# The tail of a pooled-attention and adapter kernel: where the last gates and one output addition are computed

## The chip, the cores and the metric

The kernel runs on one core of a Trainium2 chip. The metric is the device time of one execution in microseconds (us), lower is better. A core has five engines that work side by side and meet at semaphores: TensorE (PE, with its weight loads as PEld), VectorE (DVE), ScalarE (ACT), GpSimd (POOL) and SyncE (SP), which here issues the DMA transfers.

## What is computed

Two steps follow one another. The first is attention against pooled keys, where keys and values are the same matrix; the second is a mixture of eight small adapters, of which each token uses its two best. Cut to what matters:

```python
kv_pool = kv.reshape(B, H//4, 4, W//4, 4, C).mean(axis=(2, 4))     # 768 rows of 128 per batch
k = v = kv_pool.reshape(B, -1, C) @ w_sr
a = softmax(q @ k.T / sqrt(C));  x = a @ v                          # B*N = 4*12288 tokens, C = 128
logits = x @ w_gate                                                 # E = 8 adapters
w = softmax(the 2 largest logits)
out = x + sum over those 2 of  w_e * ((x @ A[e]) @ B[e])            # rank 16
```

## The kernel before

The 49152 tokens are worked in 96 chunks of 512 tokens; a chunk is four slices of 128 tokens (NS = 4). The code calls the last chunk `n` (95). Each chunk goes through these stages, and several chunks are in flight at once:

- `scores`: TensorE multiplies keys and queries, ScalarE takes the exponential (L303, L304).
- `weigh`: TensorE multiplies the exponentials with the values, extended by the gate's eight columns and a column of ones (L315). Attention output, logits and the softmax denominator come out of one product.
- `normalise` (L322, L326, L333), called `tops4` in the tail (L793, L794, L799): VectorE divides by the denominator and takes the sorted logits of each token with MAX8.
- gates: the weight of the better of two adapters is a sigmoid of the difference of logits, done as a tanh. `gate` (L342 to L346) works on GpSimd for a pair of chunks; ScalarE takes the tanh; a 1 is added; adapters that were not chosen get zero.
- `gated_hidden` (L416, L419) or, for the last six chunks, `down`/`hidden` (L430, L778) and the multiplication with the gates, `apply_gate` (L442) or `gated` (L753) on VectorE: the adapters' inner products times the gates.
- `turn` or `turned`: TensorE transposes (L762, L381), and ScalarE or VectorE copies the result out of PSUM (L768, L770, L390).
- `up` (L462): TensorE multiplies with B. Then the output is x plus this: either VectorE adds in one step from PSUM (`add_rows`, L476), or ScalarE copies PSUM to SBUF (`take`, L467) and GpSimd adds x in SBUF (`add`, L471), or TensorE puts x into the PSUM bank first (`x_first`, L454) and a `take` finishes it.
- `put` (L481) sends 256 KB of output from SyncE's queue.

The schedule is written out by hand: the order of the calls in the source is the order of the instructions in each engine's own queue, and nothing is moved by a planner. Inside the main loop chunks up to 89 take their gates through a 16-bit buffer `gw_all` which is sent to DRAM and read back in another layout. The last six chunks (90 to 95) use them straight from SBUF: `gate_tanhs(p)` for pairs 45 and 46 (chunks 90 to 93) writes the tanh to a 32-bit tile `th`, and GpSimd adds 1 and writes it into `gw_all`, whose layout has the adapters outside and the slices inside, so that the eight gates of a token lie 16 bytes apart. Chunks 94 and 95 use 32-bit tiles `arg4` and `arg5` (named `r` in the trace) in which a token's eight gates lie side by side.

After the loop stands the tail, in which the last chunks are finished in an order of its own. For the last chunk, `gate_args` (L734 to L737) forms the tanh's argument and the mask, `gate_tanh` (L740) the tanh and `gate_w` the weight: on VectorE one instruction (L745), on GpSimd two (L747, L748). `gate_args` and `gate_w` take the engine as an argument. At the end `tail_ok` (L547 to L549, GpSimd) and `all_ok` (L553 on TensorE, L554 and L556 on VectorE) write the flag `bad`, which every engine loads (L881) to decide on a branch that is not taken here; then the program ends.

```python
    gate_args(n, 0, NS, nc.vector, top5, arg5, msk5)
    gate_tanh(0, NS, arg5)
    up(n - 3, mtile([P, NTOK], name="d2"))
    gated(n - 1, 0, NS, arg4, h4)
    o2 = take(n - 3)
    ...
    gate_w(0, NS, nc.vector, arg5, msk5)
    ...
    gated(n, 0, NS, arg5, h5)
    for c, o in ((n - 6, o6), (n - 5, o0), (n - 4, o1), (n - 3, o2)):
        add(c, o, nc.gpsimd)
        put(c, o)
        if c == n - 4:
            put(n - 2, o3)
    tail_ok()
```

Of the kernel before, what the change touches and what calls it, by code (L numbers as in the profile page):

```python
# [16 lines left out]
ALU = mybir.AluOpType  # L17
# [4 lines left out]
def kernel(  # L22
# [10 lines left out]
    nc = tc.nc  # L33
# [8 lines left out]
    NS = NTOK // P  # L42
# [248 lines left out]
    tt, xps, xpair, xn, gw, gin, xT, hg, hgT, hps = {}, {}, {}, {}, {}, {}, {}, {}, {}, {}  # L291
# [63 lines left out]
    def gate_tanhs(p):  # L355
        gw[p] = gw_all[:, p % 4].rearrange("p e s -> p s e")
        if p < OWN // 2:
            nc.scalar.activation(gw_all[:, p % 4], garg[p].rearrange("p s e -> p e s"), AF.Tanh,
                                 bias=0.0, scale=0.5)
        else:  # L360
            th = small.tile([P, 2 * NS, E], FP32, tag="th", name="th")
            nc.scalar.activation(th, garg[p], AF.Tanh, bias=0.0, scale=0.5)
            nc.gpsimd.tensor_scalar(gw[p], th, 1.0, None, op0=ALU.add)

# [90 lines left out]
    def up(c, bank=None):  # L457
        fresh = c not in dps
        if fresh:
            dps[c] = mtile([P, NS, P], name="d_ps") if bank is None else as_tokens(bank)  # L460
        for s in range(NS):
            mm(dps[c][:, s], columns(hgT[c], c, s), b_bf, start=(s == 0 and fresh),  # L462
               stop=(s == NS - 1), skip_group_check=True)

    def take(c, lo=0, hi=NS):
        osb = half_out()
        nc.scalar.activation(osb[:, lo:hi], dps[c][:, lo:hi], AF.Copy)  # L467
        return osb

    def add(c, osb, eng):  # L470
        eng.tensor_tensor(osb, osb, xn[c][:, :, 0:C], op=ALU.add)  # L471

    def add_rows(c, lo=0, hi=NS, osb=None, bank_=None):
        osb = half_out() if osb is None else osb
        d = dps[c][:, lo:hi] if bank_ is None else bank_
        nc.vector.tensor_tensor(osb[:, lo:hi], d, xn[c][:, lo:hi, 0:C], op=ALU.add)  # L476
        return osb

    def put(c, osb, lo=0, hi=NS, queue=None):
        t0 = c * NTOK  # L480
        (queue or nc.sync).dma_start(  # L481
            out[t0:t0 + NTOK, :].rearrange("(p s) c -> p s c", p=P)[:, lo:hi], osb[:, lo:hi])
# [17 lines left out]
    def half_out():  # L500
        if not spare:
            o = run.tile([P, 2, NS, P], FP32, tag="osb", name="osb", bufs=3)
            spare.extend([o[:, 0], o[:, 1]])
        return spare.pop(0)
# [41 lines left out]
    def tail_ok():  # L546
        nc.gpsimd.tensor_scalar(ok[:, tail], rv[:, tail], 1.0 / L_HI, None, op0=ALU.is_ge)  # L547
        nc.gpsimd.tensor_scalar(low, rv[:, tail], 1.0 / L_LO, None, op0=ALU.is_le)
        nc.gpsimd.tensor_tensor(low, low, ok[:, tail], op=ALU.mult)  # L549
# [102 lines left out]
    for c in range(2, NCH - 1):  # L652
# [17 lines left out]
        if c >= 3 and c % 2 == 1:  # L670
            gate_tanhs((c - 3) // 2)
# [54 lines left out]
    def bank(i):  # L726
        return ps_e.tile([P, NTOK], FP32, tag=f"e{i}", name=f"e{i}")

    def gate_args(c, lo, hi, eng, top, arg, msk):
        lg = xn[c][:, lo:hi, C:C + E]  # L730
        bc = [P, hi - lo, E]
        a, m = arg[:, lo:hi], msk[:, lo:hi]
        t1, t2 = (top[:, lo:hi, i].unsqueeze(2).broadcast_to(bc) for i in range(2))
        eng.tensor_tensor(a, lg, t1, op=ALU.subtract)  # L734
        eng.tensor_tensor(m, lg, t2, op=ALU.subtract)
        eng.tensor_tensor(a, a, m, op=ALU.add)
        eng.tensor_scalar(m, m, 0.0, None, op0=ALU.is_ge)  # L737

    def gate_tanh(lo, hi, arg):
        nc.scalar.activation(arg[:, lo:hi], arg[:, lo:hi], AF.Tanh, bias=0.0, scale=0.5)  # L740

    def gate_w(lo, hi, eng, arg, msk):
        a, m = arg[:, lo:hi], msk[:, lo:hi]
        if eng is nc.vector:
            eng.scalar_tensor_tensor(a, a, 1.0, m, op0=ALU.add, op1=ALU.mult)  # L745
        else:
            eng.tensor_scalar(a, a, 1.0, None, op0=ALU.add)  # L747
            eng.tensor_tensor(a, a, m, op=ALU.mult)  # L748

    def gated(c, lo, hi, g, hb):  # L750
        if c not in hg:
            new_hg(c)
        nc.vector.tensor_tensor(  # L753
            hg[c][:, lo:hi].rearrange("p s (r e) -> p s r e", e=E),
            hb.rearrange("p s (r e) -> p s r e", e=E),
            g[:, lo:hi].unsqueeze(2).broadcast_to([P, hi - lo, RK, E]), op=ALU.mult)

    def turn(src, lo, hi, bank_, store, key, act=True):

        t_ps = bank_.bitcast(BF16)[:, 0:(hi - lo) * P].rearrange("p (s c) -> p s c", c=P)  # L760
        for s in range(lo, hi):
            mm(t_ps[:, s - lo], src[:, s], id_bf, is_transpose=True,  # L762
               start=(s == lo), stop=(s == hi - 1), skip_group_check=True)
        if key not in store:
            x_or_h = ("xt", 7) if store is xT else ("ht", 4)
            store[key] = run.tile([P, NS, P], BF16, tag=x_or_h[0], name="xr", bufs=x_or_h[1])
        if act:
            nc.scalar.activation(store[key][:, lo:hi], t_ps, AF.Copy)  # L768
        else:
            nc.vector.tensor_copy(store[key][:, lo:hi], t_ps)  # L770

    def high(c):
        return xn[c].bitcast(U16)[:, :, 1:2 * C:2].bitcast(BF16)

    def hidden(c, lo, hi, bank_):
# [5 lines left out]
    n = NCH - 1  # L781
# [3 lines left out]
    top4, top5 = top[:, 0:NS], top[:, NS:2 * NS]  # L785
    pair = xpool.tile([P, 2 * NS, VW], FP32, tag="xn", name="xn")
    xn[n - 1], xn[n] = pair[:, 0:NS], pair[:, NS:2 * NS]
    arg4, msk4, arg5, msk5 = (
        small.tile([P, NS, E], FP32, tag=f"r{i}", name=f"r{i}", bufs=1) for i in range(4))
    def tops4(c, top, y):  # L790
# [7 lines left out]
        for s in range(NS):  # L798
            nc.vector.max(top[:, s], xn[c][:, s, C:C + E])  # L799

    gate_tanhs(q_ - 1)
    y4 = ps_x.tile([P, 2, 512], FP32, tag="x", name="y4")
    weigh(n - 1, 0, y4)
# [17 lines left out]
    o6 = take(n - 6)  # L821
    h2 = hidden(n - 3, 0, NS, mtile([P, NTOK], name="h2"))
    up(n - 5, bank(0))
    o0 = take(n - 5)
# [10 lines left out]
    o1 = take(n - 4)  # L835
# [4 lines left out]
    turn(hg[n - 2], 0, NS, t_bank(), hgT, n - 2)  # L840
    x_first(n - 2, fbank(0))
    turn(high(n), 0, NS, bank(0), xT, n)
    gate_args(n, 0, NS, nc.vector, top5, arg5, msk5)
    gate_tanh(0, NS, arg5)
    up(n - 3, mtile([P, NTOK], name="d2"))
    gated(n - 1, 0, NS, arg4, h4)
    o2 = take(n - 3)
    up(n - 2)
    o3 = take(n - 2)
    gate_w(0, NS, nc.vector, arg5, msk5)  # L850
    x3 = ps_e.tile([P, 2, 512], FP32, tag="y5", name="x3")
    h5 = hidden(n, 0, NS, x3[:, 0])
    gated(n, 0, NS, arg5, h5)
    for c, o in ((n - 6, o6), (n - 5, o0), (n - 4, o1), (n - 3, o2)):
        add(c, o, nc.gpsimd)
        put(c, o)
        if c == n - 4:
            put(n - 2, o3)
    tail_ok()
    turn(hg[n - 1], 0, NS, bank(1), hgT, n - 1)  # L860
    d5 = as_tokens(fbank(1))
# [143 lines left out]
```

## Time and profile before

| | before |
|---|---|
| time, median of 3 runs | 384.3 us (384.18 to 384.46) |
| profiled execution, its own time | 383.93 us |
| profiled execution, span | 382.1 us |
| instructions | 10633 |
| TensorE busy | 363.3 us (95%) |
| VectorE busy | 305.2 us (80%) |
| ScalarE busy | 311.4 us (82%) |
| GpSimd busy | 224.0 us (59%) |

The profile is of one execution; its span counts from the first instruction to the last, and its own time is 1.8 us longer than that. Starts are given in us from the start of the span. In a timeline row the columns are start, duration, engine, line of the kernel, operation, output <- inputs with partitions and elements, number of instructions, and in brackets the idle time of the engine just before and what ended it. TensorE's busy time is modelled, and a busy TensorE is not TensorE at its peak.

### The profile page before, as it was taken

To read this page: it belongs to the slowest core of one execution; us is meant where nothing else is said; L and a number is where in the kernel's file an instruction comes from. 1 tells how busy PE (TensorE), PEld (TensorE's weight loads), DVE (VectorE), ACT (ScalarE), POOL (GpSimd) and SP (SyncE) were. 2 spreads that over 40 slices of the span, in tenths; PEclk is the share of its full clock that TensorE was granted. 3 is DMA by queue.
4 is the path that set the end of the run, shared out by engine and by line. 5 is a ranking of instruction groups with operands and counts; after the bars stand their busy time and mean duration, and the time that the engine had idled before them with its cause. 6 is when DMAs were issued, how large, how long until landed. Compare 5 with 4: busy or idle time off the path is not lost.

```text
span 382.1 us, 10633 instructions
## 1 busy us (share of the span) xinstructions
PE 363.3 (95%) x3962; PEld 268.5 (70%) x3963; DVE 305.2 (80%) x955; ACT 311.4 (82%) x393; POOL 224.0 (59%) x369
## 2 busy tenths in 40 slices
PE   4889999999999999999999999999999999999983
PEld 2457667777777877777777777777776777776772
DVE  3786538787888888888888888888888888889995
ACT  1548998889888988988898899888798798888752
POOL 1012699996889787755679697754443243341253
PEclk9999999999999999999999999999999999999996
DMA  8996999999999999999999999996997898964225
GB/s 254 405 352 193 262 308 235 340 251 330 343 300 320 311 257 320 270 325 296 314 306 307 294 283 329 289 227 183 238 254 224 255 226 194 239 171 146 88 84 195
DMA packets 93466, 100.48 MB, mean 263 GB/s; under 512 B 56676, under 2 KB 56932, under 8 KB 93412
## 3 DMA queue, kind: packets, MB, share of 16 engines
q1 hardware_dynamic: 91940, 99.58, 94.9%
q8 instruction: 31, 0.51, 0.6%
q10 hardware_dynamic: 1472, 0.20, 0.3%
q14 instruction: 23, 0.19, 0.1%
HBM read 62.33 MB, written 25.90 MB: 231 GB/s over the span
## 4 chain that ended last, share of the span: by engine, by line
PE 73%; POOL 10%; DVE 7%; ACT 5%; issue 2%; DMA 2%; SPq 0%; POOLq 0%; DVEq 0%
PE xps L315 29%; PE sg L303 26%; PE d_ps L462 5%; PE t_ps L381 4%; PE h_ps L416 4%; POOL kvt L173 4%; ACT tt L304 4%; DMA kvt<-in_kv_dram 2%; POOL q L107 1%; DVE xn L326 1%; POOL kvt L177 1%; DVE ht L419 1%; PE v_ps L197 1%; POOL msk L345 1%; PE w_ps L584 1%
## 5 line engine op out<-in xcount | busy, mean ns | idle before, releaser
L304 ACT ACTIVATE tt<-sg 128x1024 f16<-128x1024 f32 x288 | 277.5, 1022 | 36.0 <-PE sg L303 35.1
L303 PE MATMUL sg<-qT,kfT 128*128 128x512 f16 x576 | 170.0, 379 | 2.4 <-ACT tt L304 1.6
L315 PEld LDWEIGHTS <-tt 128*128 128x128 f16 x2304 | 148.0, 98 | 27.0 <-DVE xn L326 17.2
L315 PE MATMUL xps<-vext,tt 128*128 128x137 f16 x2256 | 166.3, 223 | 0.0
L476 DVE TENSOR_TENSOR osb<-d_ps,xn 128x512 f32<-128x512 f32 x88 | 60.6, 691 | 32.3 <-PE d_ps L462 32.1
L342 POOL TENSOR_TENSOR arg<-xn,top 128x64 f32<-128x64 f32 x47 | 14.7, 312 | 109.2 <-DVE top L333 93.2
L326 DVE TENSOR_TENSOR xn<-xps,rinv_all 128x548 f32<-128x548 f32 x94 | 68.5, 728 | 3.3
L303 PEld LDWEIGHTS <-kfT 128*128 128x128 f16 x576 | 49.3, 98 | 26.9 <-issue 3.8
L173 POOL TENSOR_TENSOR kvt<-kvt 128x1024 f32<-128x1024 f32 x27 | 63.7, 2359 | 0.2
L419 DVE SCALAR_TENSOR_TENSOR ht<-ge,h_ps 128x512 bf16<-128x512 f16 x90 | 60.5, 672 | 2.9 <-PE h_ps L416 2.4
L107 POOL CAST q<-q 128x1024 f16<-128x1024 f32 x44 | 45.6, 1036 | 24.9 <-DMA q<-in_q_dram 24.9
L462 PEld LDWEIGHTS <-ht 128*128 128x128 bf16 x368 | 27.3, 97 | 24.7 <-DVE ht L419 3.7
L333 DVE MAX8 top<-xn 128x8 f32<-128x8 f32 x376 | 35.2, 156 | 6.3
L392 DVE COPY xt<-t_ps 128x512 bf16<-128x512 bf16 x92 | 36.7, 399 | 0.0
L381 PE MATMUL t_ps<-id_bf,xn 128*128 128x128 bf16 x376 | 36.3, 219 | 0.0
L416 PE MATMUL h_ps<-xt,a_bf 128*128 128x512 bf16 x89 | 33.7, 379 | 1.0 <-ACT tt L304 0.7
L462 PE MATMUL d_ps<-b_bf,ht 128*128 128x128 bf16 x352 | 33.6, 219 | 0.9 <-ACT tt L304 0.7
L322 DVE RECIPROCAL rinv_all<-xps 128x4 f32<-128x4 f32 x94 | 17.1, 182 | 15.4 <-PE xps L315 13.1
L381 PEld LDWEIGHTS <-xn 128*128 128x128 bf16 x376 | 26.0, 98 | 0.3
L345 POOL TENSOR_SCALAR msk<-msk 128x64 f32<-128x64 f32 x47 | 20.1, 428 | 4.1
L346 POOL TENSOR_TENSOR arg<-arg,msk 128x64 f32<-128x64 f32 x47 | 15.0, 319 | 3.9
L344 POOL TENSOR_TENSOR arg<-arg,msk 128x64 f32<-128x64 f32 x47 | 15.0, 319 | 3.7
(151 smaller groups left out, 228.4 us busy)
## 6 DMA issues: line engine op xcount, KB each, us to landing
kvt<-in_kv_dram SPq DMA_DIRECT2D x48, 512.0 KB
q<-in_q_dram SPq DMA_DIRECT2D x44, 512.0 KB
out_dram<-osb SPq DMA_DIRECT2D x44, 512.0 KB
ge<-g_h SPq DMA_DIRECT2D x45, 256.0 KB
q<-in_q_dram SPq DMA_DIRECT2D x2, 1024.0 KB
out_dram<-osb SPq DMA_DIRECT2D x8, 256.0 KB
g_h<-g_sb SPq DMA_DIRECT2D x45, 16.0 KB
qT<-q SPq DMA_TRANSPOSE x44
```

Source lines behind the costliest of these rows:

```text
L107: nc.gpsimd.tensor_copy(q16[i], q32[i].rearrange("p k n -> p (k n)"))
L173: eng.tensor_tensor(v[:, 0], v[:, 0], v[:, d], op=ALU.add)
L303: mm(sg[:, k], kfT[b][:, j * P:(j + 1) * P], qc, start=True, stop=True)
L304: nc.scalar.activation(tt[c][:, 2 * r:2 * r + 2], sg, AF.Exp, bias=0.0, scale=scale)
L315: mm(o, tt[c][:, j, s * P:(s + 1) * P], vext[b][:, j, 0:VW], start=(j == 0 and s % 2 == 0), stop=(j == NJ - 1 and s % 2 == 1), skip_group_ ...
L326: nc.vector.tensor_tensor(xn[c].rearrange("p (b s) v -> p b s v", b=2), xv, ri.rearrange("p (b s) -> p b s", b=2).unsqueeze(3).broadcast_t ...
L381: mm(columns(t_ps, c, s), src[:, s], id_bf, is_transpose=True, start=(s == 0), stop=(s == NS - 1), skip_group_check=True)
L392: nc.vector.tensor_copy(to, t_ps)
L416: mm(h_ps, a_bf, xT[c], start=True, stop=True)
L419: nc.vector.scalar_tensor_tensor(hgT[c].rearrange("p (k a) t -> p k (a t)", k=2), gE[c // 2][:, h:h + NS // 2].rearrange("p a t k -> p k ( ...
L462: mm(dps[c][:, s], columns(hgT[c], c, s), b_bf, start=(s == 0 and fresh), stop=(s == NS - 1), skip_group_check=True)
L476: nc.vector.tensor_tensor(osb[:, lo:hi], d, xn[c][:, lo:hi, 0:C], op=ALU.add)
```

## The change

Three edits, all of them at the end of the kernel:

1. For chunks 90 to 93, `gate_tanhs` adds the 1 in place in the 32-bit tile `th`, and the gates are read from there, not from the 16-bit `gw_all`.
2. The last chunk's `gate_args` and `gate_w` go from VectorE to GpSimd. GpSimd's addition for chunk n-6 and its output transfer are placed ahead of `gate_args`; the additions for n-5 and n-4 stay behind `gate_w`, with `tail_ok` after them.
3. The output of chunk n-3 is added by VectorE from PSUM (`add_rows`), in place of ScalarE's copy and GpSimd's addition. The transfers leave SyncE's queue in the order n-6, n-3, n-2, n-5, n-4, n-1, n, where it was n-6, n-5, n-4, n-2, n-3, n-1, n.

```diff
@@ gate_tanhs, chunks 90 to 93
-            nc.gpsimd.tensor_scalar(gw[p], th, 1.0, None, op0=ALU.add)
+            nc.gpsimd.tensor_scalar(th, th, 1.0, None, op0=ALU.add)
+            gw[p] = th
@@ the tail
     turn(high(n), 0, NS, bank(0), xT, n)
-    gate_args(n, 0, NS, nc.vector, top5, arg5, msk5)
+    add(n - 6, o6, nc.gpsimd)
+    put(n - 6, o6)
+    gate_args(n, 0, NS, nc.gpsimd, top5, arg5, msk5)
     gate_tanh(0, NS, arg5)
     up(n - 3, mtile([P, NTOK], name="d2"))
     gated(n - 1, 0, NS, arg4, h4)
-    o2 = take(n - 3)
+    put(n - 3, add_rows(n - 3))
     up(n - 2)
     o3 = take(n - 2)
-    gate_w(0, NS, nc.vector, arg5, msk5)
+    gate_w(0, NS, nc.gpsimd, arg5, msk5)
     x3 = ps_e.tile([P, 2, 512], FP32, tag="y5", name="x3")
     h5 = hidden(n, 0, NS, x3[:, 0])
     gated(n, 0, NS, arg5, h5)
-    for c, o in ((n - 6, o6), (n - 5, o0), (n - 4, o1), (n - 3, o2)):
+    put(n - 2, o3)
+    for c, o in ((n - 5, o0), (n - 4, o1)):
         add(c, o, nc.gpsimd)
         put(c, o)
-        if c == n - 4:
-            put(n - 2, o3)
     tail_ok()
```

## The prediction

> **What bounds the kernel now.** I read the page first. Its chain of the work that ended last gives the whole span to TensorE, with a few per cent for the others; nothing that the change touches lies in the loop that makes up this share.
>
> ```profile
> span 382.1 us, 10633 instructions
> ...
> PE 73%; POOL 10%; DVE 7%; ACT 5%; issue 2%; DMA 2%; SPq 0%; POOLq 0%; DVEq 0%
> ```
>
> The edits begin with chunk 90, and the first instruction that gets another duration starts at 361.0 us. So only the last 21 us can change, and there I asked for the chain in order of time (start, us, piece). Two of its pieces are long for what they do:
>
> ```profile
> 371.80 1.17 DVE r L734
> 372.97 1.14 DVE r L735
> ```
>
> They are the two subtractions of `gate_args` for the last chunk, each on 128x32 numbers. The timelines of VectorE and GpSimd for the same stretch show why they are long.
>
> ```profile
> 369.44 1.06 DVE L753 TENSOR_TENSOR hgs<-t_ps,gw_all 128x512 bf16<-128x512 f32 x1 [0.46 <-PE t_ps L778]
> 370.42 0.18 DVE L793 RECIPROCAL rinv_all<-y 128x4 f32<-128x4 f32 x1
> 370.63 0.73 DVE L794 TENSOR_TENSOR xn<-y,rinv_all 128x548 f32<-128x548 f32 x1
> 371.40 0.37 DVE L799 MAX8 top<-xn 128x8 f32<-128x8 f32 x4
> 371.80 1.17 DVE L734 TENSOR_TENSOR r<-xn,top 128x32 f32<-128x32 f32 x1
> 372.89 1.21 DVE L735 TENSOR_TENSOR r<-xn,top 128x32 f32<-128x32 f32 x1
> 374.14 0.19 DVE L736 TENSOR_TENSOR r<-r,r 128x32 f32<-128x32 f32 x1
> 374.36 0.18 DVE L737 TENSOR_SCALAR r<-r 128x32 f32<-128x32 f32 x1
> 374.46 0.68 DVE L753 TENSOR_TENSOR hgs<-e,r 128x512 bf16<-128x512 f32 x1
> 375.06 0.18 DVE L745 SCALAR_TENSOR_TENSOR r<-r,r 128x32 f32<-128x32 f32 x1
> 375.34 0.69 DVE L753 TENSOR_TENSOR hgs<-x,r 128x512 bf16<-128x512 f32 x1
> 376.99 0.29 DVE L770 COPY xr<-t_ps 128x256 bf16<-128x256 bf16 x1 [0.96 <-PE t_ps L762]
> 377.48 0.69 DVE L476 TENSOR_TENSOR osb<-d,xn 128x512 f32<-128x512 f32 x1 [0.19 <-PE d L462]
> 378.08 0.41 DVE L875 TENSOR_TENSOR osb<-f,xn 128x256 f32<-128x256 f32 x1
> 378.42 0.17 DVE L554 TENSOR_REDUCE last<-e 1x1 f32<-1x32 f32 x1
> 378.62 0.20 DVE L556 TENSOR_SCALAR bad<-last,tot 1x1 int32<-1x1 f32 x1
> ```
>
> ```profile
> 368.08 0.25 POOL L734 TENSOR_TENSOR r<-xn,top 128x32 f32<-128x32 f32 x1 [1.14 <-DVE top L799]
> 368.28 0.25 POOL L735 TENSOR_TENSOR r<-xn,top 128x32 f32<-128x32 f32 x1
> 368.61 0.25 POOL L736 TENSOR_TENSOR r<-r,r 128x32 f32<-128x32 f32 x1
> 368.94 0.30 POOL L737 TENSOR_SCALAR r<-r 128x32 f32<-128x32 f32 x1
> 370.01 0.29 POOL L747 TENSOR_SCALAR r<-r 128x32 f32<-128x32 f32 x1 [0.77 <-ACT r L740]
> 370.39 0.25 POOL L748 TENSOR_TENSOR r<-r,r 128x32 f32<-128x32 f32 x1
> 370.60 3.45 POOL L471 TENSOR_TENSOR osb<-osb,xn 128x512 f32<-128x512 f32 x3
> 375.15 1.18 POOL L471 TENSOR_TENSOR osb<-osb,xn 128x512 f32<-128x512 f32 x1 [1.10 <-ACT osb L467]
> 376.30 0.29 POOL L547 TENSOR_SCALAR ok<-rinv_all 128x32 f32<-128x32 f32 x1
> 376.55 0.29 POOL L548 TENSOR_SCALAR low<-rinv_all 128x32 f32<-128x32 f32 x1
> 376.93 0.25 POOL L549 TENSOR_TENSOR low<-low,ok 128x32 f32<-128x32 f32 x1
> ```
>
> L736, of the same size, takes 0.19 once GpSimd is idle. While GpSimd does its three additions (370.60 to 374.05, 1.15 each), L734 and L735 end where the second and the third addition end. Read as a lock: a VectorE instruction whose two inputs both lie in SBUF waits out a whole GpSimd addition. VectorE instructions with one input in PSUM do not wait: L794 takes 0.73 beside the first addition, and L753 takes 0.69 beside the fourth where it took 0.68 beside none. So about 2.0 us (1.17 + 1.21 − 2 × 0.19) of the last chain is this wait.
>
> [...]
>
> **Part 1, gates in 32 bits.** With gates from `gw_all` a multiplication takes 1.06 (369.44); with gates from a dense 32-bit tile the same shape takes 0.68 and 0.69. `th` has the layout of the latter, so I take 0.37 off each of four. The first two are these:
>
> ```profile
> L442 DVE TENSOR_TENSOR hgs<-h_ps,gw_all x2: 1053/1068/1084, 361.0 to 364.5; 128x512 bf16<-128x512 f32 x2
> ```
>
> They lie ahead of the wait that TensorE shows next:
>
> ```profile
> 366.79 0.38 PE L381 MATMUL e<-id_bf,hgs 128*128 128x128 bf16 x4 [0.63 <-DVE osb L476]
> ...
> 369.24 0.88 PE L315 MATMUL y<-vext,tt 128*128 128x137 f16 x12
> ...
> 377.82 0.27 PE L553 MATMUL e<-low,ones_c 128*1 128x32 f32 x2
> ```
>
> TensorE idles 0.63 there for VectorE. Two gates cheaper by 0.37 make VectorE 0.74 earlier, so this idle time goes, and TensorE, with ScalarE's copies behind it, runs about 0.65 earlier from there. The third gate's saving falls into VectorE's idle 0.46 ahead of the fourth and is worth nothing. The fourth's counts: the last product is ready at 369.24 + 0.88 = 370.12, yet L793 starts at 370.42, when the gate is done. That start can come forward by the 0.65 and by a further 0.25, and so the end of MAX8 by 0.90, from 371.77 to 370.87. The bounds are nothing, if the cheaper gates are caught by another wait, and 4 × 0.37 = 1.5. GpSimd's addition in place is off the path.
>
> **Part 2, the last chunk's gates on GpSimd, built up from its rows.**
> - Ahead of them now stands the addition for n-6. It starts when L748 ends: 370.64, less 0.65, so 369.99; with 1.18 it ends at 371.17. The logits are there at 370.87; being queued behind this addition costs the gates 0.3.
> - `gate_args` on GpSimd, by the rows of chunk n-1: the argument is ready 0.78 after the start (368.08 to 368.86), the mask 1.16 after it. That gives 371.95 and 372.33.
> - The tanh stands in ScalarE's queue behind this copy, which ends at 372.82 before, so at 372.17 now:
>
> ```profile
> 372.22 0.60 ACT L768 ACTIVATE xr<-e 128x512 bf16<-128x512 bf16 x1 [0.27 <-PE e L762]
> ```
>
> - So ScalarE, not GpSimd, starts the tanh. I allow it 0.3, to 372.5. `gate_w` as two GpSimd instructions takes 0.63 (370.01 to 370.64), against 0.18 on VectorE: 372.5 to 373.13.
> - The product with the last gates (L753, 0.69) then runs from about 373.15 to 373.84; before it ended at 376.03. That is 2.2 us earlier.
>
> **Part 3, output n-3 on VectorE.** It adds one 0.69 (as L476), placed between the two L753. From about 371.6, when the first of them ends, to 373.15 VectorE would idle for the gate, so it costs nothing; without that cover it would cost 0.7. ScalarE loses a copy and GpSimd an addition of 1.18. In SyncE's queue the transfers of n-5 and n-4 now stand ahead of the last two and behind GpSimd's last addition.
>
> **What is late next.** Two arms now reach the end.
> - VectorE's: from the end of the last L753 to the end of L875 it was 376.03 to 378.49, 2.46. From 373.84 this gives 376.3, and about 0.6 more until the last output is issued: 376.9.
> - GpSimd's: after `gate_w` come two additions (2 × 1.15 = 2.3, to 375.43), then `tail_ok` (376.30 to 377.18, 0.88, to 376.31). Before, its result lay unused until L553 at 377.82. Now L553, L554 and L556 follow at once: 0.27 + 0.17 + 0.20 and about 0.12 for three handovers, to 377.07. Before, the flag was written at 378.82.
>
> So the end passes from VectorE's chain to GpSimd's queue, by a margin of about 0.2, and the flag comes 1.75 earlier. Output n-4 is ready at 375.4 and n-1 at 376.0 (378.17 less 2.2), so n-4 holds up nothing.
>
> ```profile
> L881 SPq TENSOR_LOAD <-bad x1: 746/746/746, 379.1 to 379.1; - x1
> ```
>
> The program's end is a fixed string of SyncE's: it loads the flag at 379.1, 0.2 to 0.3 after it was written, having issued the last output until then, and the span ends 3.0 later. In the new order that issue is over before the flag, which is worth another 0.2.
>
> **Sum.** 1.75 + 0.2 = 1.95 us. The profiled execution then goes from 383.93 to 381.98. The median of the runs shown is 384.3, 0.37 above it, and taking the same off gives 382.35: I say 382.4. Without part 1 the same addition starts the gates at 371.80, the tanh waits for the copy at 372.82, `gate_w` ends at 373.76, the additions at 376.06, `tail_ok` at 376.94 and the flag comes at 377.70: 1.1 + 0.2 = 1.3 us. All the flag's slack in the old order (377.18 to 377.82, and VectorE until 378.50) is used up in both.
>
> **The rivals.**
> - *The cheaper gates do not reach the end.* The saving of part 1 is caught by a wait that I do not see, or the 0.37 comes from something other than type and stride. For it: TensorE is close to full from 367 on, so an advance has to pass three engines. Against: both causes of the 0.63 are in the rows. It gives the 1.3 us above, 383.0; between 0.8 and 1.5 in all.
> [...]
> - *The change does not do what it says*: the addition of n-6, now ahead of the gates, may wait for the transfer of an earlier output from the same buffer. But in the old order it started right behind L748 with no idle time, so its wait was over by 370.6; at most the 0.65 of part 1 is lost there, and the gain stays near 1.3. This is in the first rival's share.
>
> **How the numbers follow.** The forecast, gains from 1.5 to 2.5, gets 0.55; the first rival 0.27; the lock with about two blocked instructions, or anything else that leaves less than 0.77, 0.11; the lock with more, slower by over 0.77, 0.07. One per 500, 0.77 us, is about what a measurement of this kernel can tell from no change. So faster 0.82, same 0.11, slower 0.07. The range runs from 381.8 (2.5 less) to 383.6 (0.7 less); it takes in the forecast and the first rival.
>
> **What would show it.** Right: L442 and all L753 near 0.69; the idle time before L381 gone; L734 to L737 on GpSimd in 0.25 to 0.3 each; L753 of the last chunk starting near 373.2; the two GpSimd additions and `tail_ok` without a gap behind `gate_w`; the last busy instruction ending near 377.1; span near 380.1. The gates' rival is right if L793 of the last chunk still starts near 370.4. [...] The forecast is wrong if the flag comes later than 378.0.

## The result: 382.75 us, 1.3 us faster

| | before | changed |
|---|---|---|
| time, median (lowest to highest) | 384.06 us (383.33 to 384.46, 6 runs) | 382.75 us (382.52 to 382.88, 6 runs) |
| ratio, 95% interval | 1 | 0.9967 [0.9954, 0.9979] |
| profiled execution: time, span | 383.93, 382.1 us | 382.79, 381.0 us |

The interval is a gain of 0.8 to 1.8 us. A second comparison gave 382.61 against 384.33 us, ratio 0.9945 [0.9926, 0.9964].

The changed kernel's VectorE in the last stretch (start, duration in us, engine, line):

```profile
361.33 0.41 DVE L393 COPY xt<-t_ps 128x512 bf16<-128x512 bf16 x1
...
369.33 0.69 DVE L754 TENSOR_TENSOR hgs<-t_ps,th 128x512 bf16<-128x512 f32 x1 [0.86 <-PE t_ps L779]
370.05 0.18 DVE L794 RECIPROCAL rinv_all<-y 128x4 f32<-128x4 f32 x1
370.27 0.73 DVE L795 TENSOR_TENSOR xn<-y,rinv_all 128x548 f32<-128x548 f32 x1
371.03 0.37 DVE L800 MAX8 top<-xn 128x8 f32<-128x8 f32 x4
371.32 0.67 DVE L754 TENSOR_TENSOR hgs<-e,r 128x512 bf16<-128x512 f32 x1
372.34 0.69 DVE L477 TENSOR_TENSOR osb<-d,xn 128x512 f32<-128x512 f32 x1 [0.34 <-PE d L463]
373.57 0.69 DVE L754 TENSOR_TENSOR hgs<-x,r 128x512 bf16<-128x512 f32 x1 [0.54 <-POOL r L749]
374.82 0.29 DVE L771 COPY xr<-t_ps 128x256 bf16<-128x256 bf16 x1 [0.56 <-PE t_ps L763]
375.03 0.68 DVE L477 TENSOR_TENSOR osb<-d,xn 128x512 f32<-128x512 f32 x1
375.63 0.41 DVE L877 TENSOR_TENSOR osb<-f,xn 128x256 f32<-128x256 f32 x1
376.98 0.18 DVE L555 TENSOR_REDUCE last<-e 1x1 f32<-1x32 f32 x1 [0.93 <-PE e L554]
377.19 0.20 DVE L557 TENSOR_SCALAR bad<-last,tot 1x1 int32<-1x1 f32 x1
```

And its GpSimd:

```profile
370.49 1.18 POOL L472 TENSOR_TENSOR osb<-osb,xn 128x512 f32<-128x512 f32 x1
371.63 0.25 POOL L735 TENSOR_TENSOR r<-xn,top 128x32 f32<-128x32 f32 x1
371.83 0.25 POOL L736 TENSOR_TENSOR r<-xn,top 128x32 f32<-128x32 f32 x1
372.16 0.25 POOL L737 TENSOR_TENSOR r<-r,r 128x32 f32<-128x32 f32 x1
372.50 0.29 POOL L738 TENSOR_SCALAR r<-r 128x32 f32<-128x32 f32 x1
372.91 0.29 POOL L748 TENSOR_SCALAR r<-r 128x32 f32<-128x32 f32 x1
373.29 0.25 POOL L749 TENSOR_TENSOR r<-r,r 128x32 f32<-128x32 f32 x1
373.50 2.32 POOL L472 TENSOR_TENSOR osb<-osb,xn 128x512 f32<-128x512 f32 x2
375.79 0.29 POOL L548 TENSOR_SCALAR ok<-rinv_all 128x32 f32<-128x32 f32 x1
376.04 0.29 POOL L549 TENSOR_SCALAR low<-rinv_all 128x32 f32<-128x32 f32 x1
376.41 0.25 POOL L550 TENSOR_TENSOR low<-low,ok 128x32 f32<-128x32 f32 x1
```

The two subtractions, 1.17 and 1.21 us before, take 0.25 each. From `gate_w` on GpSimd has no gap: two additions, `tail_ok`, and VectorE sits idle 0.93 us until the result has gone through TensorE. The end has passed from VectorE's chain to GpSimd's queue.

Starts in two profiles cannot be compared directly. The loop's last copy (L392 before, L393 here) begins at 360.67 us before and at 361.33 here, though of all that stands ahead of it only one GpSimd instruction (L363), off the path, was altered. It takes no change for such a difference: six profiles of kernels that are the same up to this copy (before twice, part 2 alone, part 3 alone, parts 2 and 3, and the one with memsets below) start it from 360.67 to 361.49. So below I count from the start of the last copy. All numbers are in us and come from starts and ends in the timelines; "logits" is the end of the last chunk's MAX8, "flag" the end of the write of `bad`, "end" the span's end.

| kernel | copy starts | copy to logits | copy to flag | flag to end | copy to end |
|---|---|---|---|---|---|
| before | 360.67 | 11.10 | 18.15 | 3.27 | 21.42 |
| before, second profile | 360.72 | 11.10 | 17.51 | 3.27 | 20.78 |
| changed | 361.33 | 10.07 | 16.06 | 3.62 | 19.67 |
| changed, second profile | 361.70 | 10.08 | 16.06 | 3.63 | 19.68 |
| part 1 alone | 361.10 | 10.08 | 17.28 | 3.28 | 20.56 |
| parts 2 and 3 | 361.49 | 11.10 | 16.84 | 3.61 | 20.45 |
| part 2 alone | 360.96 | 11.08 | 18.01 | 3.77 | 21.77 |
| part 3 alone | 361.06 | 11.08 | 19.25 | 3.74 | 22.98 |

Counted so, stretches in which the same work waits for the same things agree within 0.02 us in this table, and each larger difference has a cause that can be looked for.

### The profile page after: what moved, and what is told of

Same layout as the page of the kernel before. It is cut to its first block, busy times and chain, and to the rows that moved or that the text cites. A ratio compares the mean times of both kernels' runs of the same rounds, so it can differ in the third digit from the quotient of the medians.

```text
span 381.0 us, 10632 instructions
## 1 busy us (share of the span) xinstructions
PE 362.0 (95%) x3962; PEld 267.8 (70%) x3963; DVE 301.7 (79%) x951; ACT 310.7 (82%) x392; POOL 223.9 (59%) x374
## 4 chain that ended last, share of the span: by engine, by line
PE 76%; POOL 6%; ACT 6%; DVE 5%; DMA 4%; issue 2%; SPq 1%; POOLq 0%; DVEq 0%; ACTq 0%
PE xps L315 30%; PE sg L303 27%; PE d_ps L463 5%; PE t_ps L382 5%; ACT tt L304 4%; PE h_ps L417 4%; DMA q<-in_q_dram 3%; POOL kvt L173 2%; DMA ge<-g_h 2%; DVE xn L326 1%; DVE ht L420 1%; PE v_ps L197 1%; PE w_ps L585 1%; POOL kvt L177 1%; SPq L87 1%
## 5 line engine op out<-in xcount | busy, mean ns | idle before, releaser
L477 DVE TENSOR_TENSOR osb<-d_ps,xn 128x512 f32<-128x512 f32 x88 | 60.6, 691 | 32.3 <-PE d_ps L463 32.1
L393 DVE COPY xt<-t_ps 128x512 bf16<-128x512 bf16 x92 | 36.8, 400 | 0.0
```

The costliest lines, as they stand in the source:

```text
L393: nc.vector.tensor_copy(to, t_ps)
```

## The experiments

**The parts one by one.** Timed against the kernel before in the same session:

| kernel | median us | ratio, 95% interval |
|---|---|---|
| before | 383.93 | 1 |
| part 1 alone | 382.9 | 0.9964 [0.9951, 0.9977] |
| parts 2 and 3 | 383.62 | 0.9985 [0.9973, 0.9998] |
| part 2 alone | 384.85 | 1.0027 [1.0013, 1.0042] |
| part 3 alone | 385.77 | 1.0044 [1.0031, 1.0057] |

*Part 1 alone.*

```diff
-            nc.gpsimd.tensor_scalar(gw[p], th, 1.0, None, op0=ALU.add)
+            nc.gpsimd.tensor_scalar(th, th, 1.0, None, op0=ALU.add)
+            gw[p] = th
```

> Part 1 alone on the kernel before: chunks 90 to 93 take their gates from the dense 32-bit tile; the last chunk's gates stay on VectorE and all four additions on GpSimd. Theory (part 1 reaches the end, the lock stays): the four multiplications take 0.69, what follows runs about 0.75 us earlier, GpSimd's additions too, and L734 and L735 still take 1.1 to 1.2 us each because they end with these additions; 0.75 us faster (ratio 0.998). Rival (the cheaper gates are caught by a wait further on): within 0.2 us of before.

The logits come 1.02 earlier than before and the flag 0.87; the median falls by 1.03 us (0.75 was expected). Part 1 reaches the end. The wait stays, in VectorE's timeline of this run, with the three additions from GpSimd's beneath it:

```profile
371.21 0.28 DVE L735 TENSOR_TENSOR r<-xn,top 128x32 f32<-128x32 f32 x1
371.42 1.22 DVE L736 TENSOR_TENSOR r<-xn,top 128x32 f32<-128x32 f32 x1
372.67 1.10 DVE L737 TENSOR_TENSOR r<-r,r 128x32 f32<-128x32 f32 x1
```

```profile
370.26 3.46 POOL L472 TENSOR_TENSOR osb<-osb,xn 128x512 f32<-128x512 f32 x3
```

It moved, though, from the expected pair to the second and third instruction: L735 arrives as the first addition ends and slips through in 0.28. L736 then waits out the second addition and L737 the third. Here the cost is set by the additions still to come, not by which instruction meets them.

*Parts 2 and 3 without part 1* (the diff above turned round, on the changed kernel).

> Parts 2 and 3 without part 1: the changed kernel with the gates of chunks 90 to 93 read from the 16-bit buffer again. Theory: the two small subtractions on GpSimd take 0.25 each, the flag is written 1.1 us earlier than in the kernel before, with the chain ending in GpSimd's two additions and tail_ok; 0.8 to 1.3 us faster than before (ratio 0.9967 to 0.998). [...]

GpSimd's rows for the two subtractions:

```profile
372.67 0.25 POOL L734 TENSOR_TENSOR r<-xn,top 128x32 f32<-128x32 f32 x1
372.87 0.25 POOL L735 TENSOR_TENSOR r<-xn,top 128x32 f32<-128x32 f32 x1
```

Flag 1.31 earlier than in the first profile of before, 0.67 earlier than in the second. The time missed the expected 0.8 to 1.3 us: the medians differ by 0.3, and the interval of the ratio is a gain of 0.1 to 1.0. The mechanism is there in the rows and in the flag, but it is worth less in time than against the first profile alone. The second profile of before, below, tells why.

*Part 2 alone.*

```diff
-    gate_args(n, 0, NS, nc.vector, top5, arg5, msk5)
+    add(n - 6, o6, nc.gpsimd)
+    put(n - 6, o6)
+    gate_args(n, 0, NS, nc.gpsimd, top5, arg5, msk5)
...
-    gate_w(0, NS, nc.vector, arg5, msk5)
+    gate_w(0, NS, nc.gpsimd, arg5, msk5)
...
-    for c, o in ((n - 6, o6), (n - 5, o0), (n - 4, o1), (n - 3, o2)):
+    for c, o in ((n - 5, o0), (n - 4, o1), (n - 3, o2)):
```

> Part 2 alone on the kernel before: the last chunk's gates on GpSimd behind the addition of n-6, but output n-3 still copied by ScalarE and added by GpSimd, so that three additions stand between gate_w and tail_ok. Theory (GpSimd's queue is the end now): one more addition, 1.15 us, behind the gates uses up the whole gain; the flag at about 378.8 us as before and the time within 0.4 us of before. [...]

GpSimd's row behind its `gate_w`:

```profile
373.88 3.47 POOL L471 TENSOR_TENSOR osb<-osb,xn 128x512 f32<-128x512 f32 x3
```

Three additions where the changed kernel has two (2.32): the flag comes 1.17 later than without this third (18.01 against 16.84 for parts 2 and 3). The expected sign is right, no gain from part 2 without part 3. The time is worse than the expected 0.4 at most, 0.9 us slower than before, partly since from flag to end it takes 0.5 longer (3.77). From copy to end it is 0.35 longer than the first profile of before and 0.99 longer than the second.

*Part 3 alone.*

```diff
-    o2 = take(n - 3)
+    put(n - 3, add_rows(n - 3))
...
-    for c, o in ((n - 6, o6), (n - 5, o0), (n - 4, o1), (n - 3, o2)):
+    for c, o in ((n - 6, o6), (n - 5, o0), (n - 4, o1)):
```

> Part 3 alone on the kernel before: VectorE adds output n-3 from PSUM, the last chunk's gates stay on VectorE. Theory (VectorE's chain is the end there): L734 and L735 stay at 1.1 to 1.2 us, since the additions of n-6 to n-4 still run beside them, and the new addition of 0.69 us stands in front of the last multiplication with no idle time to hide in; 0.4 to 0.7 us slower than before. Rival (GpSimd's queue was the end before, and an addition less there pays): 0.5 us or more faster.

Slower as expected, but by 1.84 us. Besides the addition of 0.68 in VectorE's chain, a wait of its own arose, in VectorE's timeline:

```profile
378.96 0.69 DVE L476 TENSOR_TENSOR osb<-d,xn 128x512 f32<-128x512 f32 x1 [0.98 <-DMA out_dram<-osb]
```

`put(n - 3)` stands ahead of `put(n - 6)` in SyncE's queue here and waits for VectorE. So n-6 leaves 15.5 us after the copy (11.1 before), and outputs n-1 and n, which take over the tile that n-7 and n-6 shared, wait until it has landed. The changed kernel sends n-6 10.4 us after the copy, ahead of n-3: the position of that `put` in part 2 is not a detail.

**What the lock is.** Do L734 and L735 wait beside any GpSimd instruction, or only beside one that reads SBUF? On the kernel before (x is left out of three outputs; one execution, 386.13 us, in which the memsets put GpSimd's last addition later):

```diff
     for c, o in ((n - 6, o6), (n - 5, o0), (n - 4, o1), (n - 3, o2)):
-        add(c, o, nc.gpsimd)
+        if c == n - 3:
+            add(c, o, nc.gpsimd)
+        else:
+            for _ in range(4):
+                nc.gpsimd.memset(o, 0.0)
```

> The kernel before, with GpSimd's first three additions (n-6, n-5, n-4) each replaced by four memsets of the same tile, which write SBUF and read nothing (x is left out of these three outputs, and what the memsets leave is zero). [...]

VectorE and GpSimd in that run:

```profile
372.32 0.19 DVE L734 TENSOR_TENSOR r<-xn,top 128x32 f32<-128x32 f32 x1
372.43 0.18 DVE L735 TENSOR_TENSOR r<-xn,top 128x32 f32<-128x32 f32 x1
372.65 0.19 DVE L736 TENSOR_TENSOR r<-r,r 128x32 f32<-128x32 f32 x1
372.88 0.52 DVE L737 TENSOR_SCALAR r<-r 128x32 f32<-128x32 f32 x1
```

```profile
371.09 6.72 POOL L859 MEMSET osb<- 128x512 f32 x12
```

With GpSimd busy throughout but writing only, the three instructions with two SBUF inputs take 0.18 to 0.19. In the kernel before the first two of them took 1.17 and 1.21 beside additions, which read and write. So they were held beside GpSimd instructions that read, and not beside these, which only write. L737, which has one SBUF input and took 0.18 in the kernel before with GpSimd idle, takes 0.52 here. The memsets are 0.56 long each, so one ends at 371.09 + 4 × 0.56 = 373.33, shortly before L737 does, at 373.40. So L737 may have waited out a memset; one instruction is thin evidence for that, and no run shows why it took 0.52.

**Why dense gates are faster.** Two kernels from the changed one, profiled in one execution each, the first with 16 bits and dense, the second with 32 bits and apart:

```diff
-            nc.gpsimd.tensor_scalar(th, th, 1.0, None, op0=ALU.add)
-            gw[p] = th
+            th16 = small.tile([P, 2 * NS, E], F16, tag="th16", name="th16")
+            nc.gpsimd.tensor_scalar(th16, th, 1.0, None, op0=ALU.add)
+            gw[p] = th16
```

> The changed kernel, but the gates of chunks 90 to 93 go into a dense 16-bit tile, a token's eight gates side by side: 16 bits kept, the distance taken away. If the distance of 16 bytes between gates makes the multiplications slow: 0.69 us each, as changed. If the 16-bit type does: 1.06 us, as before.

```diff
-            nc.gpsimd.tensor_scalar(th, th, 1.0, None, op0=ALU.add)
-            gw[p] = th
+            far = small.tile([P, E, 2 * NS], FP32, tag="far", name="far")
+            gw[p] = far.rearrange("p e s -> p s e")
+            nc.gpsimd.tensor_scalar(gw[p], th, 1.0, None, op0=ALU.add)
```

> The changed kernel, but the 32-bit gates of chunks 90 to 93 lie in the layout of the old buffer, adapters outside, so that a token's gates are 32 bytes apart: 32 bits kept, the distance put back. If the distance makes the multiplications slow: 1.06 us each or more. If the 16-bit type does: 0.69 us.

The rows for the output tile, 16 bits dense and then 32 bits apart (shortest/median/longest in ns):

```profile
L444 DVE TENSOR_TENSOR hgs<-h_ps,th x2: 685/688/692, 361.5 to 364.5; 128x512 bf16<-128x512 f32 x2
```

```profile
L444 DVE TENSOR_TENSOR hgs<-h_ps,far x2: 1081/1083/1085, 361.0 to 364.4; 128x512 bf16<-128x512 f32 x2
```

It is the distance, not the type. With the distance put back the logits are again late (copy to logits 11.16), with 16 bits dense they are not (10.08).

**The program's end.** The changed kernel without the transfers of n-5, n-4 and n-1:

> The changed kernel without the output transfers of chunks n-5, n-4 and n-1 (these rows of the output are left out). Question: SyncE's load of the flag took 1.08 us in the changed kernel and 0.75 before. Theory (the load is slower beside output transfers in flight): back to 0.75 us or less, and the program's end after the flag, 3.6 us in the changed kernel, 0.3 us shorter. Rival (the load's time has to do with something else): 1.05 to 1.1 us again.

SyncE's load of the flag (shortest/median/longest in ns), changed kernel first, then this one:

```profile
L883 SPq TENSOR_LOAD <-bad x1: 1077/1077/1077, 377.4 to 377.4; - x1
```

```profile
L882 SPq TENSOR_LOAD <-bad x1: 485/485/485, 381.7 to 381.7; - x1
```

The load takes 0.49 beside one output transfer, 0.75 before, 1.08 beside four that start within 2.1 us; flag to end is 3.03, 3.27 and 3.62. With the transfers taken away the load is shorter, so they do lengthen it. How many are in flight does not settle by how much: in the kernel with GpSimd's queue reordered, below, SyncE's load also stands beside four transfers that start within 2.1 us, and takes 0.78:

```profile
L883 SPq TENSOR_LOAD <-bad x1: 775/775/775, 376.9 to 376.9; - x1
```

In the changed kernel, moving the flag forward, into the last transfers, gave back 0.35 us of the gain. (The one execution without the three transfers took 386.46 us. It was late from the start: the loop's first copy begins at 39.76, not 35.40, and its mean granted clock was 0.990, against 0.998 and 0.997 in the two profiles of the changed kernel. Nothing that was altered runs before the tail.)

**The same two kernels again, and two that go further.** The last four ran together; the changed kernel again:

> The changed kernel again, unaltered, as the partner of the two below and for a second profile. Theory (the tail's course is fixed, and only the start of the tail moves from execution to execution): from the last copy of the loop (L393) to the flag 16.06 us again within 0.05, whatever the time of the run; 0.9954 to 0.9979 of before again.

The kernel before again:

> The kernel before again, unaltered, for a second profile. Theory: from the last copy of the loop (L392) to the flag 18.15 us again within 0.05, though the copy itself may start up to 0.8 us later than at 360.67. Rival (the change moves the loop as well): the copy starts at 360.7 again, 0.6 us before that of the changed kernel.

The tail of the changed kernel came out the same to 0.01 us, while the ratio, 0.9945, lies just outside the expected 0.9954 to 0.9979. The tail of the kernel before did not come out the same: 17.51 from copy to flag, not 18.15, although the logits and GpSimd's last instruction (16.51 after the copy both times) agree. Its copy started at 360.72, which was the rival's sign that the change moves the loop; but parts 2 and 3, with the loop of the kernel before, start it at 361.49, and the changed kernel with gates apart at 360.64, so the rival does not hold. The two profiles differ in TensorE's clock (columns: stretch, its length, busy time and count on PE, PEld, DVE, ACT, POOL, granted clock, DMA share, GB/s), first profile and then second:

```profile
375.50:376.00 0.50, 0.50 (x5) 0.50 (x4) 0.50 (x1) 0.37 (x2) 0.50 (x1) 0.50 0.28 103
376.00:377.00 1.00, 1.00 (x10) 0.94 (x10) 0.04 (x2) 0.45 (x2) 0.92 (x4) 0.50 0.56 215
```

```profile
375.50:376.00 0.50, 0.50 (x7) 0.45 (x4) 0.50 (x1) 0.38 (x2) 0.50 (x1) 1.00 0.37 135
376.00:377.00 1.00, 0.83 (x11) 0.49 (x10) 0.49 (x3) 0.72 (x2) 0.92 (x4) 1.00 0.51 201
```

TensorE's products around it, first profile and then second:

```profile
375.20 0.40 PE L762 MATMUL e<-id_bf,hgs 128*128 128x128 bf16 x4 [1.92 <-DVE hgs L753]
375.43 1.10 PE L863 MATMUL f<-xn,id_f 128*128 128x128 f32 x4
```

```profile
375.25 0.40 PE L762 MATMUL e<-id_bf,hgs 128*128 128x128 bf16 x4 [1.93 <-DVE hgs L753]
375.48 0.66 PE L863 MATMUL f<-xn,id_f 128*128 128x128 f32 x4
```

In the first execution the clock halves at 375.5, behind TensorE's idle 1.92 us, and the flag comes 0.64 us later; in the second, behind an idle time of 1.93 us, it stays at 1.00. In the profile of part 1 alone it fell too, to 0.89 in the mean of 374.00 to 375.00 and to 0.50 from 375.00 to 378.00. What decides between the two cases no run shows.

In the first profile of the changed kernel the granted clock stays at 1.00 up to 379.48, 2.5 us behind its last product. No run changed the gap alone, so that the gap is the cause is argued, not shown.

In the changed kernel the waits for the last gates are short:

```profile
366.68 0.38 PE L382 MATMUL e<-id_bf,hgs 128*128 128x128 bf16 x4 [0.26 <-DVE osb L477]
...
374.32 0.29 PE L763 MATMUL e<-id_bf,hgs 128*128 128x128 bf16 x2 [0.43 <-DVE hgs L754]
```

and the clock is at 1.00 through its last product in both its profiles.

So the kernel before has tails of 21.42 and 20.78, the changed one of 19.68 alone: a gain of 1.74 or 1.10 by execution. The medians' 1.31 lies between; those of the second comparison differ by 1.72. More than two cases occur: of 52 executions of the kernel before in the later sessions, 21 had a mean granted clock of 0.991 or 0.992 (median 384.32 us), 19 of 0.993 to 0.995 (383.97), 11 of 0.999 or 1.0 (383.86) and one of 0.988. Read as an earlier halving where the mean is lower, the order is the expected one, but the first and last median lie 0.46 apart, and each group scatters over 1.7 to 2.5 us. For parts 2 and 3 the two tails give 0.97 or 0.33; the medians give 0.31. Part 1 alone had the halved clock in its profile, as the first of before, so its tail can be compared with that one only.

Last, GpSimd's queue in another order, from the changed kernel:

```diff
     o1 = take(n - 4)
+    add(n - 6, o6, nc.gpsimd)
+    put(n - 6, o6)
     gate_w(0, NS, nc.gpsimd, arg4, msk4)
     tops4(n, top5, y5)
+    tail_ok()
...
-    add(n - 6, o6, nc.gpsimd)
-    put(n - 6, o6)
...
-    tail_ok()
```

> The changed kernel with GpSimd's queue put in another order: the addition of n-6 goes into its idle time ahead of the gate_w of n-1, tail_ok ahead of the last gate_args. Theory (behind GpSimd's queue SyncE's queue is next: three output transfers of 0.4 us each that all become ready within 0.3 us): the flag 0.9 us earlier, bounded by VectorE's last addition, but SyncE loads it only after its last issue, so the span 0.25 us shorter. Rival (the flag alone sets the end): the span 0.9 us shorter.

and with it the transfer of n-1 on ScalarE's queue:

```diff
-    put(n - 1, add_rows(n - 1))
+    r4 = add_rows(n - 1)
...
     nc.scalar.activation(o5[:, 0:2], d5[:, 0:2], AF.Copy)
+    put(n - 1, r4, queue=nc.scalar)
```

> As the run before it, and the output transfer of n-1 is issued from ScalarE's queue, after its last copy, not from SyncE's. Theory: SyncE has one issue of 0.4 us less ahead of the flag, which it loads about 0.7 us earlier than in the changed kernel; span 0.7 us shorter than changed, about 2.0 us less than before (ratio 0.995). Rival (the last transfers' landing sets the end): no shorter than with the order alone.

| | median us | ratio to before, 95% | copy to flag | flag to end | copy to end |
|---|---|---|---|---|---|
| changed again | 382.61 | 0.9945 [0.9926, 0.9964] | 16.06 | 3.63 | 19.68 |
| GpSimd reordered | 382.7 | 0.9959 [0.9937, 0.9982] | 15.03 | 4.45 | 19.48 |
| and n-1 from ScalarE's queue | 382.51 | 0.9947 [0.9926, 0.9967] | 15.04 | 4.46 | 19.50 |

The flag comes 1.03 earlier, and the end only 0.2. In the first of them SyncE still issues the last output until 0.8 after the flag; with one issue less it loads the flag 0.5 us earlier than that (0.7 earlier than the changed kernel), yet ends at the same time. The waits of SyncE in the second of the two show what took over (us in total, times, longest):

```profile
SPq L1003 <- DMA out_dram<-osb: 0.5, 1, 0.5
```

It now waits for the last outputs to land, 0.5 us here and 0.3 in the first of the two, where the changed kernel's SyncE has no such wait. The first kernel met its theory (0.2 for 0.25), the second its rival. In time neither differs from the changed kernel.

## Why the prediction was right, and where its sum was off

The forecast was 382.4 with a gain of 1.95 us; measured were 382.75 and 1.31, inside the range. The gain itself lies below the 1.5 to 2.5 that the forecast named, in the span that it gave to its first rival, although that rival's mechanism did not occur. So the range held the result partly by the room that it left for a rival that was wrong. By its steps:

- *The reading of the page*: its row gives TensorE 73% of the chain, not the whole span, and the others 27% together. And the first instruction with another duration is GpSimd's L363, which starts at 358.62 before, not one at 361.0. Nothing in the sum rests on either.
- *The lock* (2.0 us in the last chain): right, and shown. It goes when the gates are on GpSimd (0.25 each) and when GpSimd only writes (0.19 and 0.18).
- *Part 1, logits 0.90 earlier*: right, 1.03 counted from the copy. All four multiplications take 0.67 to 0.69. The rival that the saving is caught does not hold: alone it makes the kernel 1.0 us faster. That type and stride were both given as cause was half wrong; it is the stride (0.69 with 16 bits side by side, 1.08 with 32 bits apart). TensorE's wait of 0.63 at L381 did not go but shrank to 0.26, as TensorE itself came forward too.
- *Part 2 on GpSimd*: right in the durations of its instructions. The allowance for the tanh, 0.3, was a little too much (from the end of ScalarE's copy to the start of `gate_w` it took 0.19). `gate_w` ends 12.21 after the copy, where the prediction's 373.13 is 12.46.
- *Part 3 is free between the two products*: right, 0.69 in idle time, with 0.54 left ahead of the last L754. Without part 2 that cover is gone, and the part alone costs 1.8 us.
- *GpSimd's queue becomes the end, 0.2 ahead of VectorE's arm*: right, by more, since the VectorE arm was reckoned with the halved clock (last L754 to L877: 1.78 here from 374.26 to 376.04, 2.46 in the prediction). Copy to flag was 16.06 for a predicted 16.40 (377.07 less 360.67). The 0.12 for three handovers was an estimate with no row behind it; from the end of `tail_ok` (376.66) to the flag (377.39) it took 0.73, where the prediction has 0.76.
- *The fixed end, 0.2 us shorter*: wrong. It is not a fixed string. SyncE does load the flag 0.2 sooner after it is written, but the load lengthened from 0.75 to 1.08 beside the last transfers, SyncE's waits for TensorE's queue behind it grew from 0.6 to 0.9, and flag to end grew by 0.35. This term is off by 0.55. In the sum it is partly offset, by luck, by the 0.34 at the flag: against the profile that the prediction used, 1.95 became 1.74.
- *The base of the sum*: it was made against one profile, which had the halved clock in its tail. Against an execution without it the same change is worth 1.10, not 1.74. The prediction took the durations of that tail as they stood and did not ask for the clock behind them.
- *GpSimd's instructions blocked by VectorE's* (in the chances, the lock with blocked instructions: 0.11 and 0.07): did not occur. The two additions took 2.32, and the small GpSimd instructions 0.25 to 0.29, with L754 and L477 beside them.

To the change without part 1 the prediction gave 1.3 us, 1.1 of it at the flag. Parts 2 and 3 brought the flag 1.31 earlier, but flag to end grew by 0.34 there too, which leaves 0.97 of the tail against the first profile of before and 0.33 against the second; the medians differ by 0.3. From copy to end the first profile of before loses 0.86 by part 1, 0.97 by parts 2 and 3, and 1.75 by all, so the tails nearly add, against this profile only. The timed medians, 1.0, 0.3 and 1.3, add as well, but each carries an interval of about 0.5 us to either side.

## What to carry to other kernels

Look for short instructions that end exactly where another engine's long one ends: moving the short work to that other engine can pay even where each instruction is slower there (here 0.25 on GpSimd, and 0.18 to 0.19 on VectorE without the wait), as long as that engine's queue behind it is not the next end (part 2 alone lost 0.9 us, with part 3 it gained 0.3). Compare tails from a common event in both profiles, not from the start of the span, and take two profiles of the kernel that is the base. When the end of a program is brought forward, output transfers that were hidden behind it can come into its way (here 0.35 us of the gain).

## What the runs showed that I had not expected

- Behind 1.92 us of TensorE's idle time the granted clock was 0.50 in one execution (the flag 0.64 us later), and behind 1.93 us it was 1.00 in another.
- A load of one flag from SBUF by SyncE took 0.49 to 1.08 us. It was shortest without three of the transfers, though these runs show no rule for it: beside four transfers within 2.1 us it took 1.08 in one kernel and 0.78 in another.
- A VectorE multiplication of 128x512 with a small broadcast operand took 0.67 to 0.69 where a token's eight values lie side by side and 1.05 to 1.10 where they are 16 or 32 bytes apart, in 16 and in 32 bits.
- The start of the tail lay between 360.64 and 361.70 us in thirteen of the fourteen profiles of these kernels, and at 365.55 in the one without three transfers, where the loop's first copy was already 4.4 us late.
